# Last layer of a second MLP in float16 parts scaled by powers of two found on the chip, its weights' sums formed earlier and kept in DRAM

## The chip, the cores and the metric

The kernel runs on one core of a Trainium2 chip. The core's engines have queues of their own and run in order: PE (TensorE: matmuls, and weight loads, shown as PEld), DVE (VectorE), ACT (ScalarE), POOL (GpSimd) and SP (SyncE, which issues the DMAs). The metric is the device time of one execution in microseconds, as the median of several runs.

## The reference

Masked attention (4 batches, 8 heads, 576 positions, 64 wide), then two MLPs over its 2304 tokens, each 512 -> 2048 -> 512, the first with a leaky ReLU, the second with SiLU. All inputs are float32, the MLPs' weights float64 in DRAM. Cut to what matters here:

```python
attn_out = softmax(mask(scale * q @ k.T)) @ v        # per batch and head
x = attn_out.transpose(0, 2, 1, 3).reshape(2304, 512)

h = x @ w_in                                         # first MLP
x = np.maximum(0.01 * h, h) @ w_out

h = x @ moe2_w_in                                    # second MLP, "MLP2"
g = h * (1.0 / (1.0 + np.exp(-h)))
return (g @ moe2_w_out).astype(np.float32)
```

## The kernel before, in words

**Parts.** A product of two float32 matrices is computed from two parts of each: hi, a copy rounded to fp32r, and lo, the rest. Three matmuls stand for one product: hi x lo, lo x hi and hi x hi. `split` makes the parts: hi is a copy (L378 on ACT, L380 on DVE), lo a subtraction on DVE in `rest` (L389).

**MLP2** multiplies with seven products for eight (Winograd's form): each factor is cut in quarters, four sums t1 to t4 of quarters are formed, and the products m = 1, 2, 6, 7, 5, 4, 3 (in the order of `ORDER`) are put together on the way out of PSUM.

**Its first layer** is `add_first(b, i)`: three double blocks b of 768 tokens, eight pairs i of 128-row blocks of the hidden 2048, 24 units. A unit has seven products of six matmuls with 384 columns (L1712 to L1714). Its way out: `copied` takes product 1 out of its bank to a tile (ACT, L378), `op1` to `op4` on DVE add the other banks (L1737, L1740, L1744, L1748), three SiLUs follow on ACT (L1764), and three DMAs store the results in `g2` in DRAM. `bank_free` lets the next unit's product into a bank once it has been read. `x_operands(b)` loads a double block, forms t1 to t4 on DVE and splits the seven parts, which lie in the same places for every b: a part is written when the block before has used it.

**Its last layer** is `add_last(g, i)`: five groups g of tokens (four of 512, and one of 256) by eight steps i. A step has seven products of two (in the last group one) sets of three matmuls (L1875), with a 128 x 128 tile of tokens as weights and 256 columns of the layer's weights moving. All eight steps add into the same banks; after the eighth the group leaves through `copied` and `op1` to `op4` (L1891 to L1910) and four stores. `operands4(g, i)` makes a step's operands: two loads from `g2` into a ring `raw`, three sums (L1823, L1829, L1833), a split of three quarters "a" and one of four sums "s". There are three sets of areas for sums and parts (`SUMS`, `SETS`), used in turn.

**Its weights.** `convert` turns 512 float64 columns into float32: a scaled copy `cy` on ACT (L425), the low words on ACT or DVE (L433, L435), sign (L438), a shift (L442) and an add (L447) on DVE. `last_raw(f)` does it for the last layer in steps 5 to 13 of the first layer and stores the result in `w2_kept` in DRAM; `last_pair(p)` loads it again during the third double block, forms t1 to t4 and splits seven parts, in places that `add_first(2, p)` has just used.

**What sets the order.** Nothing is ordered by hand. Each piece of work is a task with a rank, the tasks it needs, and a duration for every engine that may do it; a planner (`Schedule`) runs through them and writes each engine's queue. Where `copy_on` or `on_vector` offer several engines, it chooses one. PE's tasks follow the program through `in_turn`. MLP1 leaves its accumulators through `add_second`, whose copies (L378) free the banks that MLP2's products 7, 4, 5 and 3 use.

Of the kernel before, what the change touches and what calls it, by code (L numbers as in the profile page):

```python
# [24 lines left out]
LEAK = 0.01  # L25
BLOCKS = (384, 384, 384, 384, 384, 384)
# [20 lines left out]
UNIT3, UNIT4 = 1.75, 1.21  # L47
# [3 lines left out]
LAST_FROM, LAST_TO = 5, 14  # L51
# [8 lines left out]
PR, HLR = 1344, 4608  # L60

# [178 lines left out]
def attn_mlp_mlp(  # L240
# [73 lines left out]
    def slot(k, use="r", dtype=F32R):  # L314

        for name, (first, n) in SLOTS.items():
            if first <= k < first + n:
                return area(name, use, dtype)[:, (k - first) * 2 * DM : (k - first + 1) * 2 * DM]
        return area(f"w{k}", use, dtype)
# [87 lines left out]
    def convert(src, f, sl, rk, load_rank, to=None, slow=0, lag=0):  # L407
# [8 lines left out]
        def load():  # L416
            r = raw_room().bitcast(I64)
            nc.sync.dma_start(out=r, in_=src[f, :, sl])
            d["w0"] = r.bitcast(U32).rearrange("p (n two) -> p n two", two=2)[:, :, 0]
# [10 lines left out]
        def low(e):  # L430
            d["c"] = cc_room(U32)
            if e == "ACT":
                nc.scalar.activation(half_words(0), d["w0"], AF.Copy, scale=2.0**-29)  # L433
            else:
# [13 lines left out]

        t_load = dma(raw_free, load_rank, DM * P * 8, load, after=[*raw_after, *raw_later], slow=slow, lag=lag)
# [6 lines left out]
        t_t = plan.add({"DVE": dve2x(DM) + 60}, [t_y], rk, shifted)  # L456
        t_x = plan.add({"DVE": dve(DM) + 70}, [t_w, t_c, t_t], rk, added)
        raw_users += [t_y, t_w, t_c]
        cy_users.append(t_x)
# [52 lines left out]
    class Place:  # L512


        def __init__(self, make, deps):
            self.make, self.deps, self.tile = make, deps, None

        def view(self, a, n):
            if self.tile is None:
                self.tile = self.make()  # L520
            return self.tile[:, a : a + n]

    def second_places():
# [3 lines left out]
        for k in range(LATE - 1):  # L527
            place = Place(lambda k=k: late(k), [end_of_attention])
            w2_places.extend([(place, 0), (place, DM)])
        w2_places.append((Place(lambda: late(LATE, n=DM), [end_of_attention]), 0))  # L530
        place = Place(lambda: area("xw", "r", F32R), ())
# [3 lines left out]
        while len(w2_places) < 7 * NF // 2 - 2:  # L535
            place = Place(lambda k=k: slot(k), ())
# [3 lines left out]
        place = Place(lambda: late(LATE - 1), ())  # L540
# [3 lines left out]
    def place_of(p, k):  # L544

        second_places()
        place, at = w2_places[7 * p + k]
        deps = place.deps
        if hasattr(place, "step"):
            deps = y_there[NBLK - 2][:2] if place.step is None else [steps[base + place.step].t_g2]  # L550
        return deps, (lambda n=DM, a=0: place.view(at + a, n))

    H2 = DM // 2

# [1510 lines left out]
```

## Time and profile before

| | us |
|---|---|
| median of 3 runs | 913.59 (912.38 to 913.88) |
| the profiled execution | 912.12 |
| its span | 910.4 |
| last layer of MLP2, first start to last start on PE | 720.80 to 904.97 |
| PE, DVE, ACT busy | 897.8, 781.4, 542.6 |

The profile is of one execution, and its rows count from the start of the span. A row's duration begins when the instruction starts on its engine and contains its way through it, so rows of one engine overlap; the distance from start to start is what an instruction costs its queue. Matmul ends are modelled; distances of starts are measured.

### The profile page before, as it was taken

What the parts mean: (1) busy time and instruction counts of PE and PEld (TensorE: products, weight loads), DVE (VectorE), ACT (ScalarE), POOL (GpSimd) and SP (SyncE); (2) the same over time, 40 slices, a digit from 0 to 9 for tenths busy, and PEclk for the clock granted to TensorE, in tenths of its full rate; (3) what the DMA queues carried; (4) which work ended last, traced back from release to release, by engine and by line L of the source; (5) the groups of instructions that cost most, each with busy time, mean ns of one, the idle gap of its engine ahead of it and who ended that gap; (6) DMA issues with size and microseconds to landing.
All of it is one profiled execution on the core that took longest, in us unless ns stands there. A gap on an engine that the chain in (4) does not pass through costs nothing.

```text
span 910.4 us, 18148 instructions
## 1 busy us (share of the span) xinstructions
PE 897.8 (99%) x6569; PEld 832.0 (91%) x6569; DVE 781.4 (86%) x1802; ACT 542.6 (60%) x1195; POOL 17.1 (2%) x79
## 2 busy tenths in 40 slices
PE   9999999999999999999999999999999999999997
PEld 4655569999999999999999999999999999999997
DVE  6889899998898889888828988898899999888865
ACT  7998687776666767676627656564465632131322
POOL 0000000000000000000000000000000000000000
PEclk9999999999999999999999999999999999999999
DMA  7597827766765686856535426688755545353422
GB/s 236 179 236 191 245 89 171 143 147 151 168 162 114 151 161 145 172 157 160 105 95 197 122 82 231 230 292 290 260 192 186 180 125 161 98 159 96 148 67 86
DMA packets 176042, 149.70 MB, mean 164 GB/s; under 512 B 109264, under 2 KB 154064, under 8 KB 175952
## 3 DMA queue, kind: packets, MB, share of 16 engines
q1 hardware_dynamic: 175952, 148.55, 58.9%
q8 instruction: 51, 0.84, 0.4%
q14 instruction: 39, 0.32, 0.1%
HBM read 90.70 MB, written 32.51 MB: 135 GB/s over the span
## 4 chain that ended last, share of the span: by engine, by line
PE 86%; DVE 10%; ACT 2%; issue 1%; DVEq 0%; ACTq 0%
PE acc L1474 12%; PE acc L1875 8%; PE h L1445 5%; PE s L1875 5%; PE h L1446 5%; PE h L1447 5%; PE h L1440 4%; PE s L1139 4%; PE u L1474 4%; PE x L989 3%; PE acc L1466 3%; PE acc L1712 3%; PE acc L1713 3%; PE acc L1714 3%; PE x L1875 3%; PE u L1875 3%
## 5 line engine op out<-in xcount | busy, mean ns | idle before, releaser
L1157 ACT ACTIVATE p<-s,st 128x288 f32<-128x288 f32 (+4 forms) x120 | 62.4, 522 | 44.6 <-DVE st L1149 22.8
L1502 ACT ACTIVATE g<-h 128x384 f32<-128x384 f32 x96 | 46.8, 488 | 55.6 <-PE h L1447 49.0
L1474 PE MATMUL acc<-ghi,w 128*128 128x384 f32 x255 | 66.5, 337 | 0.0
L1139 PE MATMUL s<-k,q 128*128 128x288 f32 (+5 forms) x288 | 65.4, 322 | 0.8 <-ACT p L1157 0.8
L389 DVE TENSOR_TENSOR glo<-g,ghi 128x384 fp32r<-128x384 f32 x80 | 44.2, 552 | 24.4 <-ACT ghi L378 23.8
L1171 ACT ACTIVATE hl<-p,st 128x576 f16<-128x576 f32 (+5 forms) x93 | 55.9, 620 | 15.3 <-DVE st L1167 5.4
L1176 DVE SCALAR_TENSOR_TENSOR hl<-p,st,hl 128x576 f16<-128x576 f32 (+4 forms) x96 | 59.0, 625 | 2.8 <-ACT hl L1171 2.0
L1445 PE MATMUL h<-h,w 128*128 128x384 f32 x180 | 60.7, 337 | 0.0
L1764 ACT ACTIVATE e<-e 128x384 f32<-128x384 f32 (+1 forms) x72 | 42.7, 627 | 27.2 <-DVE e L1737 21.5
L1447 PE MATMUL h<-h,w 128*128 128x384 f32 x160 | 53.6, 335 | 0.0
L1446 PE MATMUL h<-l,w 128*128 128x384 f32 x160 | 53.6, 335 | 0.0
L1139 PEld LDWEIGHTS s<-k,q 128*128 128x128 f32 x288 | 48.0, 188 | 5.1 <-ACT p L1157 1.9
L425 ACT ACTIVATE cy<-raw 128x512 f32<-128x512 f32 x64 | 42.9, 670 | 10.6 <-DVE cc L447 4.9
L1474 PEld LDWEIGHTS acc<-ghi,w 128*128 128x128 f32 x255 | 45.6, 188 | 0.8
L378 ACT ACTIVATE ghi<-g 128x384 fp32r<-128x384 f32 x77 | 40.2, 522 | 1.2
L1474 PE MATMUL acc<-glo,w 128*128 128x384 f32 x120 | 40.2, 335 | 0.0
L1149 DVE TENSOR_REDUCE st<-s 128x1 f32<-128x320 f32 (+3 forms) x72 | 36.4, 505 | 2.4 <-PE s L1139 0.2
L989 PEld LDWEIGHTS <-vp 128*64 128x64 f16 x1296 | 31.5, 111 | 7.2 <-issue 7.2
L1445 PEld LDWEIGHTS h<-h,w 128*128 128x128 f32 x180 | 33.8, 188 | 0.2
L1440 PE MATMUL h<-h,w 128*128 128x384 f32 x96 | 33.8, 495 | 0.0
L378 ACT ACTIVATE h<-raw 128x768 fp32r<-128x768 f32 (+1 forms) x16 | 12.5, 781 | 34.8 <-PE acc L1875 30.6
L1712 PE MATMUL acc<-h,w 128*128 128x384 f32 x96 | 32.2, 335 | 1.0 <-ACT l L378 1.0
(386 smaller groups left out, 2872.1 us busy)
## 6 DMA issues: line engine op xcount, KB each, us to landing
raw<-w SPq DMA_DIRECT2D x64, 512.0 KB, 4.9
raw<-g SPq DMA_DIRECT2D x64, 256.0 KB, 3.1
g<-e SPq DMA_DIRECT2D x48, 192.0 KB, 3.1
g<-e SPq DMA_DIRECT2D x24, 384.0 KB, 3.2
kqr<-kq_l SPq DMA_DIRECT2D x16, 480.0 KB, 3.7
kqr<-kq_l SPq DMA_DIRECT2D x16, 416.0 KB, 3.8
v<-vL SPq DMA_DIRECT2D x16, 320.0 KB, 3.2
y<-yT SPq DMA_DIRECT2D x12, 384.0 KB, 3.9
```

The source lines that it names most:

```text
L989: nc.tensor.matmul(o[i * D : (i + 1) * D, c], v[i][part][:, j], p[i][a], start=start and t == 0, stop=stop and t == len(terms) - 1,)
L1139: nc.tensor.matmul(s[:, :w], hd.q[:, a : a + P], hd.k[:, k0:k1], start=i + j == 0, stop=i == len(hds) - 1 and j == 1,)
L1157: nc.scalar.activation(p[:rows, k0:k1], u.s[piece][:rows, :w], AF.Exp, bias=nm[:rows], accum_out=s2[:rows, piece : piece + 1])
L1171: nc.scalar.activation(hl[:rows, 0, :n], p[:rows], AF.Copy, scale=rc[:rows])
L1176: nc.vector.scalar_tensor_tensor(hl[:rows, 1, :n], p[:rows], rc[:rows], hl[:rows, 0, :n], op0=ALU.mult, op1=ALU.subtract)
L1440: nc.tensor.matmul(h, w[:, c * P : (c + 1) * P], x_hi[0][:, c, : s.n], start=c == 0, stop=c == NC - 1)
L1445: nc.tensor.matmul(h, w1_lo[s.f][:, sl], hi[:, c, : s.n], start=c == 0, stop=False)
L1446: nc.tensor.matmul(h, w1_hi[s.f][:, sl], lo[:, c, : s.n], start=False, stop=False)
L1447: nc.tensor.matmul(h, w1_hi[s.f][:, sl], hi[:, c, : s.n], start=False, stop=c == NC - 1)
L1474: nc.tensor.matmul(s.acc[c][:, : s.n], a, b, start=s.f == 0 and i == 0, stop=s.f == NF - 1 and i == 2)
L1712: nc.tensor.matmul(o, wlo[:, w], xhi[:, x], start=k == 0, stop=False)
L1875: nc.tensor.matmul(o, a[:, x], b, start=i == 0 and j == 0 and q == 0, stop=i == NP - 1 and q == 2, skip_group_check=True,)
```

## The change

**Parts.** The operands and weights of the last layer become two float16 parts. Both are multiplied by a power of two first: hi is an activation with a pointer to the factor (L591, ACT alone), lo one `scalar_tensor_tensor` on DVE (L596). Matmuls (now L2055) stay three for a product, with a separate weight load before each, as the order shows. On the way out the inverse factor is a pointer operand of each operation (L2073, on ACT L2079).

**Ranges.** The factors come from the largest sum of squares: each SiLU result is squared on ACT by 384 columns with `accum_out` (L1937), 96 times, the converted weights 16 times by 512 (L687). All squares write one PSUM tile. `find_range` reduces, transposes by DMA and computes the factor with DVE operations on one column; there are four ranges, three of double blocks and one of the weights.

**Weights.** `last_raw(p)` now takes a pair, in steps 1 to 12, and forms t1 to t4 there; four pieces (3 x 512 and 256 columns) are stored, and `last_pair` loads, scales and splits these. `convert` has a `joint` form for MLP2's weights: shift and add in one operation.

**Places and order.** t4 of `x_operands` is formed in place, after part 2 is split. The evacuation of MLP1's first two accumulators waits for the first cut of the block (`cut_done`) instead of both. A group's first two steps begin together: products 1, 2, 6 of step 0, then of step 1, then the rest of each. `SUMS`, `SETS` and the rooms of loads are other areas.

```diff
-UNIT3, UNIT4 = 1.75, 1.21
+UNIT3, UNIT4 = 1.75, 1.10
-LAST_FROM, LAST_TO = 5, 14
+LAST_FROM, LAST_TO = 1, 14
...
+        def joined(e):
+            d["x"] = d["c"].bitcast(F32) if to is None else to()
+            nc.vector.scalar_tensor_tensor(
+                d["x"].bitcast(U32), d["y"].bitcast(U32), 3, d["c"],
+                op0=ALU.logical_shift_left, op1=ALU.bitwise_or,
+            )
...
+    def scaled_split(n, value, parts, by, deps, rk, gate=0):
+        def high(e):
+            if e == "ACT":
+                nc.scalar.activation(parts()[0], value(), AF.Copy, scale=by())
...
+        def low(e):
+            nc.vector.scalar_tensor_tensor(
+                parts()[1], value(), by(), parts()[0], op0=ALU.mult, op1=ALU.subtract
+            )
+        hi = plan.add(high_on(n), deps, rk, high)
+        lo = plan.add({"DVE": dve(n, 1)}, [hi], rk, low)
...
+            def squared(e, di=di, f=2 * p + i):
+                nc.scalar.activation(h_all, di["x"], AF.Square, scale=SQUARE, accum_out=sum_at(64 + f))
...
+        t = ranges["most", k] = plan.add({"DVE": dve(cols[1]) + 40}, [*deps, *emptied("t2")], rk, most)
+        t = plan.add({"ACT": act(P), "DVE": 170}, [t, last], rk, spread)
+        t = dma([t, last], SHORT + rk, 40320, turned, 1200, lag=PT_LAG)
+        t = ranges["last"] = plan.add({"DVE": dve(P) + 90}, [t], rk, topped)
+        t_half = plan.add({"DVE": 160}, [t], rk, halved)
+        t = plan.add({"DVE": 130}, [t_half], rk, inverted)
+        t = plan.add({"DVE": 130}, [t], rk, ranged)
+        t_back = plan.add({"DVE": 130}, [t_half], rk, turned_back)
...
+        for k, n in enumerate((DM, DM, DM, H2)):
...
+                d["x"] = room[:, :n]
+                nc.sync.dma_start(out=d["x"], in_=w2_kept[p][:, k * DM : k * DM + n])
...
+            t_split = users[k] = scaled_split(
+                n, lambda d=d: d["x"], lambda hi=hi, lo=lo, n=n: (hi(n), lo()), by,
+                [t_in, t_range, *deps, *more, *free], rk,
+            )
...
+            cut_done.update({c: s.t_g2 for c in cs})
-            t = plan.add(copy_on(n, True), [s.t_g2, *free], GATE + rk, evac, after)
+            t = plan.add(copy_on(n, True), [cut_done[c], *free], GATE + rk, evac, after)
...
         def t4(e):
-            d["t"] = raw_room()[:, :TWO]
-            rest(e, d["t"], b21(), t2_())
+            rest(e, b21(), b21(), t2_())
-        t_4 = plan.add(on_vector(TWO), [t_2, t_in[2], *t_free], rk, t4, t_after)
+        t_4 = plan.add(on_vector(TWO), [t_2, *ts2], rp, t4)
...
+            for at in range(0, m, n):
+                def squared(e, out_=out_, at=at, col=b % 2 * 32 + i * 4 + len(t_sq)):
+                    nc.scalar.activation(
+                        h_all[:, :n], out_()[:, at : at + n], AF.Square, scale=SQUARE, accum_out=sum_at(col)
+                    )
+                t_sq.append(plan.add({"ACT": act(n) + 150}, [tg, *emptied("t2"), *([ranges["most", 1]] if b == 2 else ())], rk + 1, squared))
+        e3_free[k] = [t2, *there, *t_sq]
...
-            t[m] = in_turn(3 * subs * mm(H2), deps, rk, product)
+            t[m] = in_turn(3 * subs * mm16(H2), deps, rk, product)
...
+        def added(out_, banks_, by, more, op=ALU.add):
+            nc.vector.scalar_tensor_tensor(out_, banks_, by(), more, op0=ALU.mult, op1=op)
...
-                    last_pair(i, unit3(b, i) + 1, [t])
+                    last_pair(i, GATE + unit4(0, i) - 4, [t])
...
-            add_last(g, i)
+            if i == 0:
+                add_last(g, 0, ORDER[:3])
+                add_last(g, 1, ORDER[:3])
+                add_last(g, 0, ORDER[3:])
+            else:
+                add_last(g, i, ORDER[3:] if i == 1 else ORDER)
```

What the planner makes of it, at three places. On DVE, at the passage from the second double block to the third, before (x, xw, h, l are places of parts; L389 splits, L1740 to L1748 and L1737 are op2 to op4 and op1, L435 is a conversion, L1823 a sum of the last layer):

```order
L389 TENSOR_TENSOR xw<-t_6555,xw 128x768
L435 TENSOR_SCALAR cc<-raw 128x512
L1740 TENSOR_TENSOR g<-acc,e 128x768
L389 TENSOR_TENSOR h_1784<-y,h_1784 128x768
L1744 TENSOR_TENSOR e<-acc,g 128x768
L1748 TENSOR_TENSOR e_8003<-u,g 128x384
L389 TENSOR_TENSOR l_1785<-t_6514,l_1785 128x768
L389 TENSOR_TENSOR h_804<-raw,h_804 128x768
L1737 TENSOR_TENSOR e<-s,s_8001 128x768
L1823 TENSOR_TENSOR t_6514<-raw 128x512
L389 TENSOR_TENSOR l_805<-y,l_805 128x768
```

and after (L392 for L389, L1901 to L1912 for op1 to op4):

```order
L392 TENSOR_TENSOR xw<-t_6534,xw 128x768
L1904 TENSOR_TENSOR g<-acc,e 128x768
L392 TENSOR_TENSOR y<-y,t_6534 128x768
L1908 TENSOR_TENSOR e<-acc,g 128x768
L1912 TENSOR_TENSOR e_8097<-u,g 128x384
L392 TENSOR_TENSOR h_1776<-y,h_1776 128x768
L1901 TENSOR_TENSOR e<-s,s_8088 128x768
L392 TENSOR_TENSOR l_1777<-t_6492,l_1777 128x768
L392 TENSOR_TENSOR h_796<-y,h_796 128x768
L392 TENSOR_TENSOR l_797<-y,l_797 128x768
```

The conversion and the sum have left this stretch, t4 (`y<-y,t_6534`) has come in, and op1 stands three splits ahead of the end instead of one.

On ACT, about one unit near the end of the first layer, before (L1764 SiLU, L378 hi parts and, from x, `copied`):

```order
L1764 ACTIVATE e<-e 128x768
L1764 ACTIVATE e_8353<-e_8353 128x384
L1764 ACTIVATE e<-e 128x384
L378 ACTIVATE w_1332<-l 128x256
L378 ACTIVATE w_1333<-l 128x512
L378 ACTIVATE w_1349<-t 128x512
L378 ACTIVATE w_1350<-l 128x512
L378 ACTIVATE s_8421<-x 128x384
```

and after (L1928 SiLU, L591 hi parts, L1937 squares, L381 `copied`):

```order
L1928 ACTIVATE e<-e 128x768
L1928 ACTIVATE e_8392<-e_8392 128x384
L381 ACTIVATE s_8405<-x 128x384
L591 ACTIVATE w_8415<-t_6492,t_6534 128x512
L591 ACTIVATE w_8419<-t_6534 128x256
L1937 ACTIVATE h,t_6534<-e 128x384 x2
L1937 ACTIVATE h,t_6534<-e_8392 128x384
L591 ACTIVATE w_8441<-l,t_6534 128x512
L591 ACTIVATE w_8451<-l,t_6534 128x512
L1928 ACTIVATE e<-e 128x384
L1937 ACTIVATE h,t_6534<-e 128x384
```

The four squares of a unit (each with a read of its accumulator, which the order does not list) stand among SiLUs and hi parts; the hi parts are as many, with a pointer.

On PE, at the start of the last layer, before:

```order
L1875 MATMUL x<-w_6319,cc 128x256 x2
L1875 MATMUL x<-w_6319,y 128x256
L1875 MATMUL x<-w_6319,cc 128x256 x2
L1875 MATMUL x<-w_6319,y 128x256
L1875 MATMUL s<-w_6264,cc 128x256 x2
```

and after:

```order
L2055 LDWEIGHTS y
L2055 MATMUL x<-w_8368,y 128x256
L2055 LDWEIGHTS y
L2055 MATMUL x<-w_8368,y 128x256
L2055 LDWEIGHTS y
```

Each matmul stays as it was but for its type, and has an instruction for its weights ahead of it.

## Rows read from the trace of the kernel before

**Rows 1.** The page: engines' busy time, and the chain that ended last

```profile
PE 897.8 (99%) x6569; PEld 832.0 (91%) x6569; DVE 781.4 (86%) x1802; ACT 542.6 (60%) x1195; POOL 17.1 (2%) x79
...
PE 86%; DVE 10%; ACT 2%; issue 1%; DVEq 0%; ACTq 0%
```

**Rows 2.** Windows: length; busy PE, PEld, DVE, ACT, POOL; clock; DMA share; GB/s

```profile
662.00:720.80 58.80, 58.80 (x339) 58.54 (x338) 57.94 (x99) 33.74 (x62) 0.00 (x0) 1.00 0.55 189
720.80:758.00 37.20, 36.27 (x299) 35.82 (x299) 36.92 (x64) 14.84 (x20) 0.00 (x0) 1.00 0.43 136
758.00:796.00 38.00, 38.00 (x318) 37.89 (x317) 33.14 (x47) 9.37 (x11) 0.00 (x0) 1.00 0.42 127
```

**Rows 3.** Timeline, PE: start, duration, engine, line, tiles, [idle before, releaser]

```profile
548.00 0.45 PE L1712 MATMUL acc<-h,w 128*128 128x384 f32 x1 [0.96 <-ACT l L378]
...
549.90 0.44 PE L1712 MATMUL acc<-l,w 128*128 128x384 f32 x1 [0.58 <-ACT l L378]
...
668.57 0.34 PE L1712 MATMUL u<-l,w 128*128 128x384 f32 x1
...
720.80 0.40 PE L1875 MATMUL x<-w,cc 128*128 128x256 f32 x2
...
734.74 0.39 PE L1875 MATMUL acc<-w,l 128*128 128x256 f32 x1 [0.89 <-DVE l L389]
...
886.16 0.50 PE L1875 MATMUL acc<-w,h 128*128 128x256 f32 x2 [0.81 <-DVE e L1905]
...
904.97 0.52 PE L1875 MATMUL u<-w,y 128*128 128x256 f32 x3
```

**Rows 4.** Chain that ended last: start, duration, engine, tile, line, count

```profile
888.94 1.08 PE acc L1875 x9
...
905.17 0.70 DVE l L1901
...
905.90 0.69 DVE e L1905
```

**Rows 5.** Timeline, PE, mask fills in float16: all nine, last two, next

```profile
9.76 2.12 PE L1277 MATMUL h<-hl 128*128 128x512 f16 x9
...
11.28 0.59 PE L1277 MATMUL h<-hl 128*128 128x512 f16 x2
11.71 0.27 PE L1393 MATMUL pt<-e 128*128 128x128 f32 x1
```

**Rows 6.** Line L1277, its weight loads: minimum, median, maximum ns

```profile
L1277 PEld LDWEIGHTS <-hl x26: 95/98/99, 5.7 to 17.6; 128*128 128x128 f16 x26
```

**Rows 7.** Groups of DVE by line and form: count, busy us, mean ns, idle

```profile
L389 DVE TENSOR_TENSOR w<-l,w 128x512 fp32r<-128x512 f32 x19 | 12.9, 680 | 0.0
...
L1176 DVE SCALAR_TENSOR_TENSOR hl<-p,st,hl 128x512 f16<-128x512 f32 x16 | 11.9, 748 | 1.0 <-ACT hl L1171 0.9
...
L442 DVE TENSOR_SCALAR cy<-cy 128x512 uint32<-128x512 uint32 x64 | 26.3, 415 | 4.0 <-ACT cy L425 3.8
```

**Rows 8.** Timeline, DVE: the last low part at the second passage

```profile
667.84 0.95 DVE L389 TENSOR_TENSOR l<-y,l 128x768 fp32r<-128x768 f32 x1
```

**Rows 9.** Timeline, ACT: activations that read their accumulator

```profile
204.10 0.49 ACT L1157 ACTIVATE p<-s,st 128x288 f32<-128x288 f32 x1
204.48 0.20 ACT L1157 ACTIVATION_READ_ACCUMULATOR p<-s,st 128x1 f32 x1
204.57 0.50 ACT L1157 ACTIVATE p<-s,st 128x288 f32<-128x288 f32 x1
```

**Rows 10.** Groups of ACT by line and form, columns as in rows 7

```profile
L1764 ACT ACTIVATE e<-e 128x384 f32<-128x384 f32 x48 | 24.9, 518 | 22.6 <-DVE e L1737 21.5 <-DMA g<-e 1.1
L1764 ACT ACTIVATE e<-e 128x768 f32<-128x768 f32 x24 | 20.2, 844 | 4.6 <-issue 2.6 <-DVE e L1744 1.7
...
L378 ACT ACTIVATE w<-l 128x512 fp32r<-128x512 f32 x20 | 12.1, 620 | 3.4 <-DVE l L389 3.4
...
L1171 ACT ACTIVATE hl<-p,st 128x512 f16<-128x512 f32 x15 | 10.7, 717 | 3.7 <-ACT p L1157 2.0 <-DVE st L1167 1.0 <-DMA kqr<-kq_l 0.7
```

More of the change, by code (lines that the diff above doesn't have):

```diff
@@ L60 @@
 PR, HLR = 1344, 4608
+SQUARE, RANGE = 2.0**-16, 2.0**-68
 class Both(float):
@@ L431, in low @@
             d["c"] = cc_room(U32)
-            if e == "ACT":
+            if e == "ACT" and joint:
+                nc.scalar.activation(half_words(0), d["w0"], AF.Copy, scale=LOW, bias=-0.5)
+            elif e == "ACT":
                 nc.scalar.activation(half_words(0), d["w0"], AF.Copy, scale=2.0**-29)
+            elif joint:
+                nc.vector.tensor_scalar(half_words(0), d["w0"], 2.0**-29, -0.50001, op0=ALU.mult, op1=ALU.add)
             else:
@@ new lines, in last_raw, with store @@
+        t_3 = plan.add(on_vector(H2), [t_1, in1, t_sq[0]], rk, t3)
+        t_4 = plan.add({"DVE": dve(H2)}, [t_2, *d1["raw"]], rk, t4)
+        pieces = (
+            (0, DM, lambda: d1["x"], in1), (1, DM, lambda: d["t"], t_2),
+            (2, DM, lambda: d0["x"], t_3), (3, H2, lambda: d1["r"][:, :H2], t_4),
+        )
+        for k, n, value, t in pieces:
+            def store(k=k, n=n, value=value):
+                nc.sync.dma_start(out=w2_kept[p][:, k * DM : k * DM + n], in_=value())
+            there.append(dma([t], SHORT + rk, P * n * 4, store, lag=LAG))
@@ new lines, in find_backs, with product, negative @@
+    def find_backs():
+        for k in range(NBLK // 2):
+            c, minus = (lambda i=16 + 2 * k + j: scalar_at(i) for j in (0, 1))
+            rk = unit3(NB3 - 1, 0) + 5 + k
+            def product(e, k=k, c=c):
+                nc.vector.tensor_scalar(c(), ranges[k][3](), ranges[3][3](), None, op0=ALU.mult)
+            def negative(e, k=k, c=c, minus=minus):
+                nc.vector.tensor_scalar(minus(), c(), -1.0, None, op0=ALU.mult)
+            t = plan.add({"DVE": 160}, [ranges[k][1], ranges[3][1]], rk, product)
+            t_minus = plan.add({"DVE": 130}, [t], rk, negative)
+            ranges["c", k] = c, minus, [t, t_minus]
@@ L1594, in attn_mlp_mlp @@
     g2 = [[dram.tile([P, 2, TWO], F32, name=f"g2_{i}_{b}") for b in range(NB3)] for i in range(NP)]
-    w2_kept = [dram.tile([P, DM], F32, name=f"w2k{f}") for f in range(NF)]
+    w2_kept = [dram.tile([P, 4 * DM], F32, name=f"w2k{p}") for p in range(NP)]
     def bank(m, n):
@@ L1792, in operands4 @@
         d = {}
-        free, after, users = raws.next()
+        odd = n < TOK and i % 2
+        free, after, users = ((), raws.takers[-1:], raws.users[-1]) if odd else raws.next()
         t_in = []
```

286 lines of the change are left out of this document (186 added, 100 removed).

## The prediction

> **What bounds the kernel now.** I read the page first: TensorE is busy for 99% of the span, VectorE for 86% and ScalarE for 60%, and 86% of the chain that ended last is PE's [rows 1]. So the time is PE's stream of matmuls plus its stalls. A gain comes from matmuls that start at shorter distance, a loss from operands that come late. The windows say where that can happen: the granted clock is 1.00 throughout, which is the 2.4 GHz level, and DVE is busy for 57.94 of the last 58.80 us of MLP2's first layer, 36.92 of the next 37.20 us, and 33.14 of 38.00 us afterwards [rows 2]. There is little room beside PE when the two layers meet, and some in the last layer.
>
> The last layer runs from 720.80 to 904.97 + 3 x 0.12 = 905.33 us [rows 3], 184.5 us. It has 40 steps: 32 of 7 x 6 matmuls and 8 of 7 x 3, 1512 in all, and nine of them take 1.08 us on the chain [rows 4], 120 ns each. Its 256 columns at 2.4 per ns are 106.7 ns, so 13.3 ns of each lie over the columns. 1512 x 0.120 = 181.4 us; two stalls, 0.89 us at 734.74 (operands of the third step) and 0.81 us at 886.16 (a bank that DVE frees late) [rows 3], make 1.7; the 1.4 us left are hitches too small to place. Behind the last matmul two DVE operations and a store end the span [rows 4].
>
> **The change, part by part.**
>
> *Matmuls in float16.* No matmul of these operands in float16 is in this trace, but the mask fills of L1277 are float16, with weights of 128 x 128 loaded before every one, and 512 columns. The last two start at 11.28 and PE's next matmul at 11.71 [rows 5]: 215 ns for 213.3 ns of columns. From the first, at 9.76, all nine take 1.95 us, 216.7 each. So 1.7 to 3.4 ns lie over the columns, where the fp32r form has 13.3. I take 2.7: 109.4 ns, and 1512 x 0.1094 = 165.4 us, 16.0 less. The ends for 1.7 and 3.4 are 163.9 and 166.5. Should the 13.3 stay, nothing is saved.
>
> In float16 the weight load is an instruction of its own ahead of each matmul. In the fills it takes 98 ns [rows 6] and costs nothing beyond the 2 to 3 ns: loads of 98 ns and 213 ns of columns are done every 215 ns, one under the other. In the new layer the same load has only 106.7 ns of columns to lie under. 98 is still less, with 9 ns to spare.
>
> The Trainium skill speaks against this: the page "TensorE: Matmul & The Clock Gate", section "The mechanism", says that a weight load overlaps matmuls in flight only when it goes to another row group. Every load here uses all the rows; by that rule each would stand open. The fills disagree with it: by the rule they would be 213 + 98 = 311 ns apart, and are 215. What it would give is the third rival below.
>
> *Stalls of the last layer.* The areas of the first steps' operands are changed, so that the third step no longer waits for one that comes free late: 0.89 us go. A group now begins with products 1, 2, 6 of its first two steps, so six products instead of three run before bank 7 is wanted. In the last group that is 6 x 3 x 0.109 = 2.0 us of cover against 1.1, more than the missing 0.81. Against this, the evacuation's four operations read a pointer, which on DVE costs 0.07 us each (748 against 680 ns at 512 columns [rows 7]). I leave 0.3 us for these places. DVE's own load in a group: sums, lows and evacuation come to about 31.4 us of the 8 x 42 x 0.1094 = 36.8 us that PE needs, 85%, against 33.14 of 38.00 before [rows 2]; PE stays the bound. Last layer: 165.4 + 1.4 + 0.3 = 167.1, **17.4 us less**.
>
> *Start of MLP2.* PE waited 0.96 and 0.58 us at 548.00 and 549.90 for ScalarE's evacuation of MLP1's last banks [rows 3]. That evacuation now waits for the first cut of the block alone, 6 x 0.173 = 1.04 us earlier. Bounds: all 1.5 us, or none if another operand is as late; nothing in the rows is, so **-1.5 us**.
>
> *Passages between double blocks.* t4, 768 columns, moves from the early part of the operands to between the splits; one such operation takes 0.95 us as recorded, some 0.87 from start to start. At the second passage the last low part starts at 667.84 and is there at 668.79 [rows 8], while PE would read it at 668.57 [rows 3]: the margin is already gone. By the order, 0.87 us enter ahead of it and 0.95 us (a conversion and a sum) leave, but op1 moves forward too, to where it may have to wait for its third product, with the splits queued behind it. Bounds: 0, and 2 x 0.87 = 1.7 for both passages. I take the middle, **+0.9 us**.
>
> *Squares on ScalarE.* 96 squares of 384 columns and 16 of 512 are new, each with a read of its accumulator. An activation of 288 columns is followed by its read 0.38 us later, and the next activation starts 0.09 us on [rows 9]; so a read costs 0.09, and an activation's record exceeds its start-to-start time by 0.11. From 518 and 844 ns for silu at 384 and 768 columns, 620 for a copy of 512, and 717 with a pointer [rows 10]: 0.41, 0.74, 0.51 and 0.61 us. A square is 0.41 + 0.09, and since all write one tile, each waits for the one before: 0.14 more, 0.64. In the last five units of the first layer (7 products of 6 matmuls of 0.173 = 7.28 us each, 36.4 us) the order now holds 20 squares 12.8, 15 silus 7.8, 28 highs of last operands and weights 17.1, and 4 copies 1.5: 39.2 us, where it had 19. **ScalarE is 2.8 us over.** DVE, counted in the same way, has 30.8 us of work in the last four units, of 29.1. What hides it: the order puts late squares behind the highs, the ranges of the third double block are wanted only in the fourth group of the last layer, and a unit's first bank has about 4 us before its late evacuation reaches PE. What it costs without that cover: 2.8 us. Bounds 0 and 2.8; I take **+1.2**, since DVE queues behind ScalarE here and has no slack.
>
> *What is covered.* The weights' sums move into the first layer's steps 1 to 12. Each of the 32 conversions of MLP2's weights loses its shift, 0.415 us as recorded [rows 7], to the operation that adds; by the order, DVE's total in the first layer falls by some 3 us. Queue SP gets 31 more DMAs and 4 transposes; the kept sums add about 3.1 MB each way, some 9 us of all DMA engines over the layer's 24 x 7.28 = 175 us, where they are busy 0.55 [rows 2]. The chains that find ranges (reduction, transpose, small DVE operations of 0.15 us) end units before they are used. Bounds for all these -0.5 and +1; I take 0. *Tail:* two more pointers, **+0.2**.
>
> **Sum.** The profiled execution took 912.12 us. 912.12 - 17.4 - 1.5 + 0.9 + 1.2 + 0.2 = 895.5. The median of the runs is 1.5 above that execution, so **897.0 us**. Its own range, from the bounds above, is 893 to 902.
>
> **Rivals.**
>
> 1. *ScalarE bounds the first layer.* Then what exceeds a unit falls on PE: at the passages the order gives it 8.9 and 8.3 us of 7.28 (2.6 over), at the end 2.8, and DVE 1.7 more: 7.1 us in place of my 0.9 + 1.2. 897.0 + 5.0 = 902. For it: in-order engines, and silus that wait 22.6 us for DVE today [rows 10]. Against: ScalarE's 39.2 us are an excess of 8%, for five units only.
> 2. *The 13.3 ns are not the type's.* If they belong to loading new weights for each 256 columns, all 16.0 us stay: 913.0, no change. Against: the fills load new weights each time too.
> 3. *The weight load shows; slower.* L2055's loads have 9 ns to spare at most. If a load does not lie under the matmul before it, it adds up to 98 ns: 1512 x 0.098 = 148, 1045 us. It decides early: 11 ns of each load (16.6 / 1512) take the whole gain, and 20 ns give 897 + 30 = 927. For it: such loads under only 107 ns of columns are not in the rows. Against: the fills hide theirs whole.
>
> The rule of the Trainium skill named above is the full form of this third rival; the trace agrees with it nowhere that I read.
>
> **How the numbers follow.** Forecast 0.72, first rival 0.17, second 0.05, third 0.04, and 0.02 for a mixture between 904 and 911. The range 893 to 904 takes the forecast's own, less its thin ends, and the first rival: about 0.8. Faster by over 0.2% (1.8 us, about what a measurement of this kernel can tell from no change): 0.72 + 0.17 + 0.01 = 0.90; the same 0.05; slower 0.05.
>
> **What would show it.** Matmuls of the last layer 109 to 110 ns apart, and the layer 167 us from its first start to its last end: the main step. 120 ns: the second rival; over 125: the third. No wait on ScalarE near 548 us; no stall over 0.3 us at a third step or a group's start. In the first layer's last five units, PE's idle time and who released it: more than 3 us, released by ScalarE or by DVE behind it, is the first rival. The forecast is wrong above all if the end of the first layer starves PE beyond 2.8 us, or if a load of 98 ns under 107 ns of columns is too tight.

## The result, and the profile after

The changed kernel takes 898.48 us as the median of its runs (897.39 to 899.35), against 913.74 us (912.38 to 914.75) of the kernel before: a ratio of 0.9833, 95% interval 0.9816 to 0.985. The forecast was 897.0 us, in a range of 893 to 904. The profiled execution took 897.39 us with a span of 895.7, 14.7 us less than the one before. It divides like this (starts of PE's matmuls, in us; the last matmul's end is its start and one distance):

| stretch | before | after | difference |
|---|---|---|---|
| to MLP2's first matmul | 541.67 | 543.32 | +1.65 |
| MLP2's first layer, to the last layer's first start | 179.13 | 181.11 | +1.98 |
| last layer, to the end of its last matmul | 184.53 | 166.19 | -18.34 |
| from there to the end of the span | 5.06 | 5.07 | 0.0 |

The page's busy times and its chain by engine, after:

```profile
PE 882.3 (99%) x6569; PEld 796.9 (89%) x6569; DVE 775.9 (87%) x1794; ACT 626.8 (70%) x1428; POOL 17.8 (2%) x81
...
PE 81%; DVE 11%; ACT 4%; DMA 2%; issue 2%; SPq 0%; DVEq 0%; ACTq 0%
```

PE is still the bound ([rows 1]: 99% of the span), ScalarE has 84 us more to do. Windows of the stages of [rows 2], the first of them cut to the last 19.40 us ahead of the last layer (length; busy PE, PEld, DVE, ACT, POOL; clock; DMA share; GB/s):

```profile
705.00:724.40 19.40, 19.22 (x111) 18.77 (x109) 18.60 (x28) 19.24 (x40) 0.00 (x0) 1.00 0.69 232
724.40:761.00 36.60, 36.12 (x331) 32.21 (x330) 36.49 (x59) 26.73 (x46) 0.00 (x0) 1.00 0.62 192
761.00:798.00 37.00, 37.00 (x340) 33.00 (x338) 34.86 (x52) 16.49 (x17) 0.00 (x0) 1.00 0.49 150
```

At the end of the first layer ScalarE and VectorE are full together (19.24 and 18.60 of 19.40 us), and VectorE stays full through the last layer's first group. The chain, and the weight loads of the last layer's line:

```profile
878.01 0.98 PE acc L2055 x9
...
890.49 0.76 DVE l L2073
...
891.28 0.75 DVE e L2073
```

```profile
L2055 PEld LDWEIGHTS <-y x525: 95/98/102, 724.4 to 890.4; 128*128 128x128 f16 x175
```

Nine matmuls take 0.98 us where they took 1.08 [rows 4]; 98 ns of load under 106.7 ns of columns cost nothing. Between starts there are 109 ns 1250 times and 110 ns 249 times, of 1511. PE's stalls after, as a timeline:

```profile
550.20 0.44 PE L1876 MATMUL acc<-h,w 128*128 128x384 f32 x1 [1.51 <-ACT l L381]
...
552.11 0.44 PE L1876 MATMUL acc<-l,w 128*128 128x384 f32 x1 [0.58 <-ACT l L381]
...
669.92 0.44 PE L1877 MATMUL acc<-l,w 128*128 128x384 f32 x1 [0.57 <-DVE l L392]
...
720.15 0.45 PE L1876 MATMUL acc<-h,w 128*128 128x384 f32 x1 [0.18 <-DVE e L1908]
...
725.74 1.47 PE L2055 MATMUL s<-w,y 128*128 128x256 f16 x12 [0.48 <-DVE e L1901]
```

Against [rows 3]: the last layer's stalls of 0.89 and 0.81 us are gone, but for 0.30 us at the last group's start (874.24). The pair at MLP2's start, which I had counted as gone, is there, and its first part is longer. A new one is at the second passage. (Below, a stall's cost is the whole excess of the distance between two starts over its usual value; with the hitch, that is the 0.1 us by which the matmul behind the stalled one is late as well, the pair costs 2.64 us after and 2.09 before.)

### The profile page after: what moved, and what is told of

Same layout as the page of the kernel before. It is cut to its first block, busy times and chain, and to the rows that moved or that the text cites. A ratio compares the mean times of both kernels' runs of the same rounds, so it can differ in the third digit from the quotient of the medians.

```text
span 895.7 us, 18467 instructions
## 1 busy us (share of the span) xinstructions
PE 882.3 (99%) x6569; PEld 796.9 (89%) x6569; DVE 775.9 (87%) x1794; ACT 626.8 (70%) x1428; POOL 17.8 (2%) x81
## 4 chain that ended last, share of the span: by engine, by line
PE 81%; DVE 11%; ACT 4%; DMA 2%; issue 2%; SPq 0%; DVEq 0%; ACTq 0%
PE acc L1640 11%; PE acc L2055 8%; PE s L2055 5%; PE h L1611 5%; PE h L1612 5%; PE h L1613 5%; PE s L1305 4%; PE u L1640 4%; PE h L1606 4%; PE x L1155 3%; PE u L2055 3%; PE x L2055 2%; PE acc L1876 2%; PE acc L1877 2%; PE acc L1632 2%; PE acc L1878 2%
## 5 line engine op out<-in xcount | busy, mean ns | idle before, releaser
L392 DVE TENSOR_TENSOR glo<-g,ghi 128x384 fp32r<-128x384 f32 x80 | 44.3, 553 | 20.4 <-ACT ghi L381 19.9
L1611 PE MATMUL h<-h,w 128*128 128x384 f32 x180 | 60.7, 337 | 0.0
L2055 PEld LDWEIGHTS <-y 128*128 128x128 f16 x525 | 51.2, 98 | 6.8 <-issue 0.8
L1613 PE MATMUL h<-h,w 128*128 128x384 f32 x160 | 53.6, 335 | 0.0
L2055 PEld LDWEIGHTS <-x 128*128 128x128 f16 x492 | 48.1, 98 | 6.0 <-issue 0.5
L1928 ACT ACTIVATE e<-e 128x384 f32<-128x384 f32 (+1 forms) x72 | 42.4, 622 | 9.0 <-DVE e L1908 8.7
L1937 ACT ACTIVATE h<-e 128x384 f32<-128x384 f32 x96 | 46.8, 488 | 1.7
L381 ACT ACTIVATE ghi<-g 128x384 fp32r<-128x384 f32 x75 | 39.1, 522 | 1.2
L1315 DVE TENSOR_REDUCE st<-s 128x1 f32<-128x320 f32 (+3 forms) x72 | 36.4, 505 | 2.2
```

The costliest lines, as they stand in the source:

```text
L1611: nc.tensor.matmul(h, w1_lo[s.f][:, sl], hi[:, c, : s.n], start=c == 0, stop=False)
L1613: nc.tensor.matmul(h, w1_hi[s.f][:, sl], hi[:, c, : s.n], start=False, stop=c == NC - 1)
L2055: nc.tensor.matmul(o, a[:, x], b, start=i == 0 and j == 0 and q == 0, stop=i == NP - 1 and q == 2, skip_group_check=True,)
```

## The experiments

### Where the 1.65 us ahead of MLP2 come from

Nothing that the change speaks of runs in the attention stage. But the early evacuation (`cut_done`) is a dependency of every block, and the planner answers with another order from the end of MLP1's block 1 on (the engines' orders part at 224 us). Four kernels take it apart.

```diff
-            t = plan.add(copy_on(n, True), [cut_done[c], *free], GATE + rk, evac, after)
+            t = plan.add(copy_on(n, True), [s.t_g2, *free], GATE + rk, evac, after)
```

> The changed kernel with the evacuation of MLP1's accumulators waiting for the whole block again (the cut_done part undone). Theory: the early evacuation let the planner write another order for the attention stage, and that order costs the 1.65 us by which the second MLP starts later (543.32 against 541.67 us). With it undone, PE's order up to the last layer is that of the kernel before, so the second MLP should start at 541.7 again and the time fall by 1.6 us, less what the stall at MLP2's start gains or loses (2.09 us before, 2.64 us after). Rival: the 1.65 us come from other parts (joint conversions, weights' sums); then the start stays at 543.3 and the time at 898.5.

The kernel before with the early evacuation as its only change:

```diff
+        cut_done = {}
...
+            cut_done.update({c: s.t_g2 for c in cs})
...
-            t = plan.add(copy_on(n, True), [s.t_g2, *free], GATE + rk, evac, after)
+            t = plan.add(copy_on(n, True), [cut_done[c], *free], GATE + rk, evac, after)
```

> The kernel before with the early evacuation alone. Theory: the attention stage loses 1.65 us, so the second MLP starts at 543.3; the stall at its start is 1.13 + 0.75 us and its two hitches in the kernel before and falls by at most 1 us, since ScalarE's order still has the SiLU and its table load ahead of the evacuation. Time 914 to 915.5. Rival, my prediction's own step: the stall goes and nothing else changes, 912.2.

The early evacuation for the last block of MLP1 alone:

```diff
-            t = plan.add(copy_on(n, True), [cut_done[c], *free], GATE + rk, evac, after)
+            t = plan.add(copy_on(n, True), [cut_done[c] if blk == NBLK - 1 else s.t_g2, *free], GATE + rk, evac, after)
```

> The changed kernel with the early evacuation in the last block of MLP1 alone. Theory: attention as in the kernel before, the second MLP starts at 541.7; one bank's evacuation now stands ahead of the table load on ScalarE, so the first of the two stalls goes and the second stays at about 0.75 us. Against the changed kernel 1.65 + 1.9 = 3.5 us less, 895. Rival: the waits are not for the place in ScalarE's order; then only the 1.65 us go, 896.8.

The same, with two banks on VectorE and all four ahead by rank:

```diff
-            t = plan.add(copy_on(n, True), [cut_done[c], *free], GATE + rk, evac, after)
+            t = plan.add(
+                {"DVE": dve_psum(n)} if blk == NBLK - 1 and c > 1 else copy_on(n, True), [cut_done[c] if blk == NBLK - 1 else s.t_g2, *free], GATE + rk - (2 if blk == NBLK - 1 else 0), evac, after)
```

> As the kernel with the early evacuation in the last block alone, with all four evacuations ahead of the SiLU: two on ScalarE before its table load, two on VectorE. Theory: both stalls at MLP2's start go, some 0.8 us less than that kernel, 894.3. Rival: the table load and the SiLU come later by as much and the stall returns at op1's successors; no gain, 895.

Measured, in this order: 894.65 us (ratio to the kernel before 0.9799, 0.9783 to 0.9815), 917.1 (1.0046, 1.0031 to 1.0061), 901.57 (0.9873, 0.9859 to 0.9888) and 895.34 (0.981, 0.9795 to 0.9824). The first gained more than the 1.6 us I gave it, the second and the third came out above both of their figures, and the fourth shows no gain over the 895 that its rival gave.

The start of MLP2 alone does not tell, since the first loads of a run arrive up to 1 us apart and a few waits before 175 us differ. So I compared PE's 1301st and 3901st matmul (209.0 and 517.9 us before), which frame the attention stage, with the kernel before; shifts in us, for all kernels of this study:

| kernel | order of attention | at the 1301st | at the 3901st | gained in between |
|---|---|---|---|---|
| changed kernel | new | 0.02 | 1.65 | 1.63 |
| before_early_banks | new | 1.13 | 2.74 | 1.61 |
| after_no_squares | new | 0.60 | 2.22 | 1.62 |
| after_128_columns | new | 0.38 | 2.00 | 1.62 |
| after_squares_twice | new | 1.13 | 2.97 | 1.84 |
| after_all_banks_wait | as before | 0.91 | 0.87 | -0.04 |
| after_early_banks_last | as before | 0.58 | 0.57 | -0.01 |
| after_banks_first | as before | 0.36 | 0.34 | -0.02 |
| after_mlp1_end_sooner | as before | 1.25 | 1.21 | -0.04 |
| sooner_splits_first | as before | 1.21 | 1.21 | 0.0 |
| sooner_splits_weights_later | as before | 0.25 | 0.25 | 0.0 |
| after_banks_wait_old_products | as before | 0.78 | 0.74 | -0.04 |

That is settled: the order that the early evacuation makes in the attention stage costs 1.6 us (1.8 in after_squares_twice), whatever else a kernel has. What in that order costs them is open: PE's idle time in this stretch of the changed kernel is 0.2 us. In the kernel before, with nothing else changed, the early evacuation gives 4.2 us away; besides the attention's 1.6, the profiled execution has a stall of 1.50 us (0.89 before) at the last layer's third step, and behind it matmuls at the lower clock for 3.6 us.

### Why the stalls at MLP2's start did not go

My step was that the copies could begin when the first cut ends. The direct test is before_early_banks, which has that edit alone. Its stalls at MLP2's start, in PE's timeline, are those of [rows 3], 0.96 and 0.58 us:

```profile
550.74 0.44 PE L1714 MATMUL acc<-h,w 128*128 128x384 f32 x1 [0.96 <-ACT l L378]
...
552.64 0.44 PE L1714 MATMUL acc<-l,w 128*128 128x384 f32 x1 [0.58 <-ACT l L378]
```

The reason shows in another kernel. In after_banks_first, the two copies of ScalarE stand at the head of its queue and need only the first cut by the code. PE's last matmul of MLP1, the copies, and the product that waits for them, in its timelines of PE and ScalarE:

```profile
547.04 0.34 PE L1640 MATMUL u<-glo,l 128*128 128x384 f32 x1
548.34 0.44 PE L1877 MATMUL acc<-h,w 128*128 128x384 f32 x1 [0.96 <-ACT l L381]
```

```profile
547.41 0.87 ACT L381 ACTIVATE l<-acc 128x384 f32<-128x384 f32 x2 [1.58 <-PE u L1640]
```

ScalarE sits idle for 1.58 us and is released by the second cut's last matmul. So the copies begin no earlier than they did. The semaphore events in the traces say more: of MLP1's last twelve matmuls, six of each cut, only the last one is followed by an update of PE's semaphore, at 547.39 us here, at 547.05 in the kernel before and at 548.70 in the changed kernel. The end of the first cut gave no signal, and there was nothing earlier to wait for.

That a wait can go by more than the bank it needs could have been read in the kernel before, in ScalarE's timeline:

```profile
547.08 0.87 ACT L378 ACTIVATE l<-acc 128x384 f32<-128x384 f32 x2
549.36 0.49 ACT L378 ACTIVATE l<-acc 128x384 f32<-128x384 f32 x1 [1.41 <-PE acc L1714]
```

PE's last matmul of MLP1 there ends at 547.04, and the copies follow at 547.08, as this kernel's code has it. But both pass before product 7 starts at 548.00 [rows 3], though it needs one bank, and the third copy waits for product 7, whose bank is another. Three of the four banks are one tile, `acc`; that these waits go by the tile and not by the bank is how I read the rows, no run takes the tile apart. It doesn't explain the missing signal: the last matmul of MLP1 writes the fourth bank, tile `u`, and in after_banks_first the last one into `acc` starts at 546.52, 0.52 us ahead of it. Why no signal stands at an earlier matmul is open.

In the changed kernel something else came on top. ScalarE's timeline:

```profile
546.89 0.66 ACT L429 ACTIVATE cy<-raw 128x512 f32<-128x512 f32 x1
547.57 1.28 ACT L1928 ACT_TABLE_LOAD   x1
548.87 0.52 ACT L1928 ACTIVATE e<-e 128x384 f32<-128x384 f32 x1
549.30 0.85 ACT L381 ACTIVATE l<-acc 128x384 f32<-128x384 f32 x2
```

PE's last matmul of MLP1 ends at 548.69. The table load and the first SiLU, earlier and hidden in the kernel before, now lie behind it, and the copies behind them: they begin at 549.30, 0.60 us after the signal, where they began 0.03 us after it before.

In after_early_banks_last this went wrong the other way: one copy ran ahead of the table load, at 547.65, but the product waited for the second, behind it, at 549.88: a stall of 2.79 us, and then a granted clock of 0.50, the lower of the two levels, until after 557.5. The stall costs 3.1 us where I expected none and the lower clock 2.8; with 1.4 us more than the changed kernel loses at the passages and behind, this is why its time is 6.6 us above what I expected.

What does help is work for PE in that time. On after_all_banks_wait:

```diff
-BEHIND, LAG = 6, 2500
+BEHIND, LAG = 2, 2500
```

> The changed kernel with the evacuation waiting for the whole block again, and with MLP1's last matmuls ahead of MLP2's third product instead of behind it. Theory: the stall at MLP2's start is not one of ScalarE's place in the queue alone: the copies begin only when MLP1's last matmul ends, and PE has nothing to do meanwhile; with a product of 1.04 us between, the first stall (1.91 us in the kernel with the block's wait) shrinks to under 0.5 and the second (0.75) goes. 894.65 - 2.2 = 892.4. Rival: MLP1's last operands are not there by then and PE waits for these instead; 894.6.

895.82 us (0.981, 0.9795 to 0.9825). In this kernel's PE timeline the pair of stalls is down to one of 0.30 us, as expected:

```profile
548.55 0.44 PE L1876 MATMUL acc<-h,w 128*128 128x384 f32 x1 [0.30 <-ACT l L381]
```

The time did not follow, since this order again has stalls of 0.74 us at both passages (609.04 and 668.31, DVE's L392), and of 0.49 and 0.85 at 704 and 720 (DVE's L1908), which after_all_banks_wait does not have.

### What stalls a passage

The changed kernel has t4 in the passage and a stall; after_all_banks_wait has t4 there and none. VectorE's timelines, of the changed kernel and of after_all_banks_wait (L1901 is op1, L1912 op4):

```profile
666.58 0.55 DVE L1912 TENSOR_TENSOR e<-u,g 128x384 f32<-128x384 f32 x1
667.04 0.94 DVE L392 TENSOR_TENSOR h<-y,h 128x768 fp32r<-128x768 f32 x1
668.05 0.96 DVE L1901 TENSOR_TENSOR e<-s,s 128x768 f32<-128x768 f32 x1
668.92 0.95 DVE L392 TENSOR_TENSOR l<-t,l 128x768 fp32r<-128x768 f32 x1
```

```profile
666.30 0.55 DVE L1912 TENSOR_TENSOR e<-u,g 128x384 f32<-128x384 f32 x1
666.76 0.95 DVE L392 TENSOR_TENSOR l<-t,l 128x768 fp32r<-128x768 f32 x1
667.63 0.95 DVE L1901 TENSOR_TENSOR e<-s,s 128x768 f32<-128x768 f32 x1
668.50 0.94 DVE L392 TENSOR_TENSOR h<-y,h 128x768 fp32r<-128x768 f32 x1
```

In the first, op1 starts 0.14 us after the split ahead of it could have released it (667.04 + 0.87 = 667.91), and the low part l is there at 669.87, when PE has waited since 669.35. In the second that part is finished at 667.71. So op1's place makes the stall, with t4 in the stretch in both. The test, on the kernel with MLP1's end sooner:

```diff
-        rp = rk if b == 0 else SHORT + unit3(b, 0) - 1
+        rp = rk if b == 0 else GATE + unit3(b, 0) - 0.5
```

> As the kernel with MLP1's last matmuls sooner (895.8), with the splits of a new double block ranked ahead of that block's own evacuation on VectorE, so that op1 no longer stands between them. Theory: the passages' stalls (0.74 us with 0.28 of hitches at 609 and 668 there) come from op1, which waits for its third product with the last splits queued behind it; both go, 2.0 us less, 893.8. Rival: t4's 0.87 us in that stretch make the last split late wherever op1 stands; then the stalls stay, 895.8.

894.48 us (0.9798, 0.9783 to 0.9812). Both stalls are gone, with t4 still there; hitches of 0.18 us remain. A kernel without t4 in the stretch was not run: by the count its 0.87 us, too, would have been enough for l to be there in time (669.00).

On this kernel:

```diff
-                    last_pair(i, GATE + unit4(0, i) - 4, [t])
+                    last_pair(i, GATE + unit4(0, i) - 2, [t])
```

> As the one before, with the last layer's weights split at a lower rank, behind the evacuation of the first layer's last units. Theory: the stalls at 704 and 720 (0.49 and 0.85 us with 0.2 of hitches, PE waiting for op3) come from weights' low parts that stand ahead of op3 on VectorE; they go too, 1.5 us less, 892.3. Rival: the weights then come late for the last layer's first steps, and PE waits there; no gain, 893.8 or more.

894.61 us (0.9798, 0.9783 to 0.9812): no gain, and the stall near 702 us is as long as it was (0.84 us, and 0.86 in sooner_splits_first). This is no test of my theory there: VectorE's order is the same in both kernels up to 706 us, and two low parts still stand between op1 and op3. The rank moved nothing ahead of this stall. VectorE's and ScalarE's timelines ahead of it:

```profile
697.55 0.75 DVE L596 SCALAR_TENSOR_TENSOR w<-l,t,w 128x512 f16<-128x512 f32 x1 [1.33 <-ACT w L591]
```

```profile
694.99 0.48 ACT L1937 ACTIVATE h<-e 128x384 f32<-128x384 f32 x1
...
695.63 0.49 ACT L1937 ACTIVATE h<-e 128x384 f32<-128x384 f32 x1
...
696.29 0.50 ACT L1937 ACTIVATE h<-e 128x384 f32<-128x384 f32 x1
...
696.81 1.94 ACT L591 ACTIVATE w<-l,t 128x512 f16<-128x512 f32 x3
```

Three squares, 0.64 and 0.66 us from start to start, stand ahead of the high parts for which VectorE waits 1.33 us. Behind this wait come op1, a low part, op2, a low part and op3, and PE loses 0.84 us at 702.28. So ScalarE's squares have a part in this stall, and the two low parts (0.66 us each) may have one too; which of the two would do alone was not tried. It is the first rival's mechanism, once, at about a tenth of its price.

### What the squares cost

```diff
...
-                    nc.scalar.activation(
-                        h_all[:, :n], out_()[:, at : at + n], AF.Square, scale=SQUARE, accum_out=sum_at(col)
-                    )
+                    pass
...
```

(The `...` stands for two edits that let the ranges be found without these sums: a constant for them, and one more task to wait for.)

> The changed kernel with the 96 squares of SiLU results left out (the sums they would give are set to a constant), everything else in the same order on every engine. Theory: the stalls at the end of the first layer and behind it (0.45 us at 720.15 and 0.65 us at 725.74 in the changed kernel, with their hitches) come from a ScalarE that is full there, and DVE behind it; both go, 1.1 us less, 897.4. The passage's 0.85 us at 669.92 is DVE's and stays. Rival: they come from DVE's own queue; then nothing changes, 898.5.

899.77 us (0.9851, 0.9834 to 0.9869). The stalls at the end stay: 1.31 us at 723.96, for VectorE's op3, and 1.06 at the passage. My theory fell. The run isn't the clean test that I wanted, since VectorE's order is another one from 614 us on; in it the stall of 0.65 us behind the layer's end is gone, and the one ahead of it is longer. But it shows the cause: from 713 to 723 us VectorE is busy for 10.00 of 10 us and ScalarE for 6.33. In the changed kernel VectorE is busy for all 9.50 us from 713 to 722.5, and waits for ScalarE once in the last 19.40 us of the layer, 0.6 us at 706. So these stalls are of VectorE's own queue, as the rival said. The profiled execution loses 1.6 us to the lower clock at 553, of which below.

```diff
+                    for _ in (0, 1):
+                        nc.scalar.activation(
+                            h_all[:, :n], out_()[:, at : at + n], AF.Square, scale=SQUARE, accum_out=sum_at(col)
+                        )
```

> The changed kernel with each of the 96 squares done twice. By my prices a square takes 0.64 us of ScalarE, and ScalarE has 159 us of work in the first layer's 24 x 7.28 = 175 us; 96 more make 220 us. Theory: ScalarE then bounds the layer, PE waits for it, and the time rises by about 45 us, to 943. Rival: ScalarE has more room than that because squares fill times in which it waits for DVE anyway; under 15 us more.

939.61 us (1.0285, 1.0269 to 1.0301), 41 us more than the changed kernel for 45 expected. PE's excess over its usual distances grows by 33.4 us in the first layer and 5.3 in the last; some 4 and 1.5 us of these are matmuls at the lower clock, behind the stalls. In MLP2's first layer ScalarE is busy for 203.93 of 215 us, against 154.49 of 181.10 in the changed kernel. So 96 more do not fit, and the 96 that the change brings do, but for the layer's end, where ScalarE is full. That a square costs 0.64 us is read from the rows above; the time alone, with the lower clock in it, doesn't give it.

### The weight load under its columns

```diff
...
-                            o, a[:, x], b, start=i == 0 and j == 0 and q == 0, stop=i == NP - 1 and q == 2,
+                        for c in (0, 1):
+                            nc.tensor.matmul(
+                                o[:, c * P : (c + 1) * P], a[:, x], b[:, c * P : (c + 1) * P],
...
```

> The changed kernel with each of the last layer's 1512 matmuls cut into two of 128 columns, each with its own weight load, in the same order. It measures how much of a load of 98 ns lies under other matmuls. Theory, from the mask fills: a load is hidden as long as it can begin under earlier matmuls, and two matmuls take 2 x 56 ns; the layer takes 3024 x 0.056 = 169.3 us, 4 us more, 902.5 in all. Rival: a load takes 98 ns of the array in any case and the 106.7 ns of columns only just covered it; then 3024 x 0.098 = 296 us, 131 us more, 1029. The Trainium skill, page TensorE: Matmul & The Clock Gate, section Back-to-back issue gap, gives about 81 ns for a sustained stream of loads and matmuls of 128 columns; by that figure, an estimate, the layer would take 245 us.

902.73 us, from one execution. Its last layer, from PE's timeline, and its loads:

```profile
726.20 0.84 PE L2056 MATMUL x<-w,y 128*128 128x128 f16 x12
...
895.60 0.50 PE L2056 MATMUL u<-w,y 128*128 128x128 f16 x6
```

```profile
L2056 PEld LDWEIGHTS <-y x1050: 95/98/102, 726.2 to 895.8; 128*128 128x128 f16 x175
```

From 726.20 to 895.60 + 6 x 0.056 = 895.94 are 169.7 us for 3024 matmuls, 56.1 ns each, with 53.3 ns of columns. The loads still last 98 ns each, and one is issued every 56: they lie under other matmuls, and under one another. So the margin of 9 ns, on which the third rival stood, is none: the record of a load is not what it takes from the stream.

By the Trainium skill's rule (TensorE: Matmul & The Clock Gate, section "The mechanism": a load overlaps matmuls in flight only where the row group differs) these loads would stand open; this run disagrees. So it does with the figure of its section "Back-to-back issue gap" for a sustained stream at 128 columns, 81 ns; the formula that the same section keeps for single matmuls, N / 2.4 + 2.5 ns, gives 55.8 and 109.2 ns, and the stream runs at 56.1 and 109.4.

### The order of products at a group's start

On after_all_banks_wait:

```diff
-            if i == 0:
-                add_last(g, 0, ORDER[:3])
-                add_last(g, 1, ORDER[:3])
-                add_last(g, 0, ORDER[3:])
-            else:
-                add_last(g, i, ORDER[3:] if i == 1 else ORDER)
+            add_last(g, i, ORDER)
```

> The changed kernel with the evacuation waiting for the whole block (894.65), and with the last layer's products in one order, step by step, instead of two steps begun together at a group's start. Theory, by my prediction's step: three products of cover are too few for op1 to op3 of the group before; at the last group PE waits 0.8 us again and at the other three 0.1 to 0.2 more, and the first group waits for its third step's sums; 1.2 us more, 895.9. Rival: with float16's free time on VectorE the three products are enough, 894.65.

900.65 us (0.9869, 0.9853 to 0.9886), 6.0 us more than after_all_banks_wait. The second and the fifth group's start, in PE's timeline:

```profile
762.56 1.47 PE L2055 MATMUL acc<-w,x 128*128 128x256 f16 x12 [1.37 <-DVE e L2073]
...
875.64 0.81 PE L2055 MATMUL acc<-w,x 128*128 128x256 f16 x6 [1.13 <-DVE e L2073]
```

All four such starts cost 1.2 to 1.5 us, 5.5 together; I had written 1.2 for the whole. In the kernel before, with the same order of products, three of them cost 0.17 and one 1.07. VectorE's timelines at the second group's start say where the difference comes from. Here it puts a split of 1.19 us between op1 and op2 and one of 0.92 between op2 and op3; in the kernel before it puts sums of 0.64 and 0.33 us there. That is 1.14 of the 1.35 us; three products of cover that are 0.19 us shorter in float16, and op2 and op3 that are 0.06 us longer each, cover the rest.

## Why the prediction held, and where its steps did not

The sum came to -16.6 us and the profiled execution gave -14.7. That it came so near is in part luck: two steps together lost 3.7 us against the forecast, and two others gave 1.65 us back. Term by term:

| step | forecast | measured |
|---|---|---|
| float16 matmuls | -16.0 | -16.0 |
| stalls of the last layer | -1.4 | -2.3 |
| start of MLP2 | -1.5 | +0.55 |
| passages | +0.9 | +0.9 |
| squares, end of the first layer | +1.2 | +0.45 |
| what is covered | 0 (-0.5 to +1) | +1.65 |
| tail | +0.2 | 0.0 |

**The main step** was right in mechanism and size: the fills' 2.7 ns over the columns [rows 5] are those of the new layer, and the load of 98 ns [rows 6] costs nothing. after_128_columns shows that it would still be hidden by a matmul half as long. This excludes the second and the third rival.

**The start of MLP2** is the step that failed. It took the wait in the code, for the first cut, to be the wait on the chip, from a row that named ScalarE as releaser. The edit alone, in before_early_banks, left both stalls as they were: PE signals once, after the second cut. And I did not price ScalarE's own order, in which a table load of 1.28 us came to lie on the path; that is the +0.55.

**What is covered** was off by 1.65 us, beyond its bound: the same edit gave the planner a reason to write another order for 300 us that nothing else of the change touches. I gave that no term of its own, and the bound of +1 us for everything hidden did not hold it. (Another figure of this step was off without harm: by the page's shares of the span the DMA engines are busy for 32 us more, not some 9, and no wait of PE comes from it.) The edit itself was worth nothing: without it, after_all_banks_wait takes 894.65 us, 3.8 less than the changed kernel, or 3.0 when each is taken against the kernel before measured beside it (913.74 and 912.95). Of these, 1.6 are the attention's; the rest are stalls at the passage and at the end of the first layer that its order happens not to have.

**The passage** came out in size, 0.92 us, and by the mechanism named, op1 with the splits queued behind it. t4's place, with which the step began, is not shown to be the cause: the stall goes while t4 stays.

**The squares**: the price of one, 0.64 us, is what the rows show. ScalarE is busy for 34.69 us of the last five units, 36.4 us, and for 19.24 of the last 19.40; my count of 39.2 us was not all done there. PE lost 0.45 us ahead of the last layer and 0.65 in it (the table counts the latter with the last layer's stalls). Together, 1.1 us, that is near the term, but by luck: their origin is VectorE's own queue, and without any squares PE loses no less. The first rival did not come.

**The last layer's stalls** gained 0.9 us more than I wrote. The 1.4 us that I had left as hitches too small to place belong to the same stalls: 0.57 us more at the third step, 0.26 more at the last group, 0.17 at each of the three other group starts and 0.10 at one more place; they went with them. The new order of products is worth far more than the 0.81 us I gave it: 5.2 us in the last layer of the run with the old one. I had priced it against the stalls of the slower layer; in the new one VectorE has splits between the evacuation's operations, the cover is shorter and the operations are longer.

**The best version** of these is one of three within their spread: after_all_banks_wait at 894.65, sooner_splits_first at 894.48 and sooner_splits_weights_later at 894.61 us, each 0.3 to 0.4% below the changed kernel (ratios 0.9799 and 0.9798 with intervals to 0.9815 and 0.9812, against 0.9833 with one from 0.9816).

## What to carry to other kernels

Price an edit to a dependency by everything that a planner may reorder for it, and look at whether the machine's wait really goes by that dependency: ask which instruction signals, and try the edit alone. An edit of rank tests nothing where the order stays the same, so compare the orders first. When the bound engine becomes faster, reckon anew what its work used to cover; a stall that the old rows do not show may be bought off by another part of the same change. A duration in a record (a load of 98 ns) is not a distance in a stream: where a price decides the sign, look for a row in which it is paced.

## What the runs showed of the hardware that was not expected

The granted clock can fall behind stalls that are short. In the changed kernel's profiled execution PE idles 1.51 and 0.58 us at 550, and the clock stays at 1.00. In after_128_columns, whose program is the same up to the last layer, the same two idles are followed by 0.50, the lower of the two levels. In after_all_banks_wait PE idles 1.75 and 0.58 us at the same place, and the clock stays at 1.00. Windows of the changed kernel, then of after_128_columns:

```profile
552.50:555.00 2.50, 2.50 (x17) 2.50 (x16) 1.51 (x3) 1.52 (x4) 0.00 (x0) 1.00 0.79 226
```

```profile
552.50:555.00 2.50, 2.50 (x8) 2.50 (x9) 1.03 (x2) 1.88 (x5) 0.00 (x0) 0.50 0.71 229
555.00:557.50 2.50, 2.50 (x15) 2.50 (x13) 1.19 (x2) 0.00 (x0) 0.00 (x0) 0.87 0.84 282
```

PE does 8 matmuls in the time of 17 (0.32 us each instead of 0.173), until about 555.6; that costs 1.5 us there, 1.6 in after_no_squares and 2.8 in after_early_banks_last, where the idle was 2.79 us. So a stall of 1.5 us can cost as much again, in some executions. It isn't all of what spreads the runs of a kernel by 1 to 2 us: the changed kernel's 897.39 and 899.35 us both have a mean granted clock of 1.0.

After a stall of PE in the first layer the second matmul starts some 0.1 us late as well (0.28 or 0.29 us behind the first instead of 0.17, as at 550.20 and 550.49 in the changed kernel), so a stall's price is its idle time and 0.26 to 0.28 us. The float16 matmuls of the last layer don't have this second part: the idle of 0.48 us at 725.74 costs 0.64, that of 1.37 us at 762.56 in after_banks_wait_old_products 1.52.
